# Thirty-two instead of thirty-six small unread products at the start of TensorE's program

## The chip, the core and the metric

The kernel runs on one core of a Trainium2 chip. The metric is device time in microseconds (us) for one launch, the median of several runs. A core has five engines with a queue of instructions each: TensorE (PE, matrix products; its weight loads are listed apart as PEld), VectorE (DVE), ScalarE (ACT), GpSimd (POOL) and SyncE (SP), which here only issues transfers (DMA).

## What is computed

Two stages in a row. The first is a linear attention over 4 batches, 4 heads, 1088 positions and 32 channels, with a feature map of products of two small projections:

```
phi(x) = (S1 x) outer (S2 x), flattened         # r = 8, so 64 features
kv  = sum_s phi(k)_s v_s ;  z = sum_s phi(k)_s
out = (phi(q) kv) / (phi(q) z + 1e-06)
```

The second is a gated layer with a mix over positions, on x = the attention's output with its heads joined (4 x 1088 x 128):

```
h = relu(x @ w_in)                              # 128 -> 1024
u, v = h[:512], h[512:]
v_n = (v - mean(v)) / sqrt(var(v) + 1e-06)
v_s = w_spatial @ v_n + b_spatial               # 1088 x 1088, over positions
out = (u * v_s) @ w_out                         # 512 -> 128
```

## The kernel before, in words

The 1088 positions are 9 tiles of 128 (the last half full). The large product with `w_spatial` is done for each batch and each of 4 blocks of 128 channels in three pieces of 424, 332 and 332 positions; float32 accuracy comes from splitting both factors in a high and a low part, so one product is three matrix products (lines 1123, 1125, 1132). ACT makes the high parts by a copy that rounds, DVE or POOL subtract them for the low parts. The weights `w_in`, `w_out`, `S1`, `S2` arrive as 64-bit numbers and DVE turns them into float32 with integer operations (lines 643 to 656).

The order of every engine's work is fixed before anything runs: a planner walks the operations with estimated costs, led by two written lists (ORDER, from line 69, and THEN, from line 100). In the first 50 us of its estimated time it also puts unread products (`fill`, line 605, the product at line 608) where it expects TensorE to wait. The planner sees the operation of this change as one item of a fixed cost, 1300 ns (line 603).

The start matters for this change. On DVE a tile `z9` is set to zero with two rows of ones (lines 591, 592). TensorE then runs 5 unread products 128x128 of it (N_WARM, line 596), and one operation that consists of many small ones (line 601): they write 32x32 results into a bank that is overwritten later, and take their place among four columns of the array in turn.

```
def small():                                                                        # line 598
    for i in range(N_SMALL):
        q = 32 * (i % 4)
        nc.tensor.matmul(wps[q:q + 32, :32], z9[:, q:q + 32], z9[:, :32],
                         start=True, stop=True, tile_position=(0, q))
op("PE", 1300, f4=True, fn=small, r=[z9], w=[wps], due=0)                            # line 603
```

Behind them in TensorE's queue come one fill and then the first products that matter, `project` (line 747): the keys (tiles `kt`, loaded by SP) times `sk`, the converted S1 and S2. Their results go by ACT (line 752) and DVE (line 754) into the features `kp`. Then 8 fills, the third group of keys, the first group of queries (tile `c`), one more fill, and the sums over keys (line 784). SP issues all transfers (line 580) in one queue; several wait until the tile that they overwrite has been read.

All products here are float32; the profile shows each of those products as two records of TensorE (the 5 of line 596 as 10, the 36 of line 601 as 72).

Of the kernel before, what the change touches and what calls it, by code (L numbers as in the profile page):

```python
# [36 lines left out]
EXP_LO = 2.0 ** -15  # L37
EXP_HI = 122879.9921875
N_WARM = 5
N_SMALL = 36  # L40


PS_BUFS = {"po": 3, "sp": 2, "pu": 1, "sd": 2}
# [456 lines left out]
def tile_kernel(ctx: ExitStack, tc: tile.TileContext, kT, qT, vA, sks, idn, msk, wT, w_in, w_out, bsp, out):  # L500
# [97 lines left out]
    def small():  # L598
        for i in range(N_SMALL):
            q = 32 * (i % 4)  # L600
            nc.tensor.matmul(wps[q:q + 32, :32], z9[:, q:q + 32], z9[:, :32], start=True, stop=True, tile_position=(0, q))
# [948 lines left out]
```

## Time and profile before

| | |
|---|---|
| device time, median of 3 runs | 325.61 us (324.69 to 326.08) |
| profiled execution, its time | 326.01 us |
| its span, first to last instruction | 324.2 us |
| granted TensorE clock, mean of the profile's record | 0.999 |
| busy PE / PEld / DVE / ACT / POOL | 317.2 / 301.8 / 226.2 / 164.8 / 64.5 us |

A busy share says how full an engine is over the span, not what the end hangs on; for the start of the program the order of time on each engine and the waits between them say more. A row of a timeline has a start, a duration, the engine, the line, the tile written and read, the shape and, behind x, the number of records that are merged in it. Idle time ahead of a row stands in brackets with what ended it.

### The profile page before, as it was taken

To read this page: it belongs to the slowest core of one execution; us is meant where nothing else is said; L and a number is where in the kernel's file an instruction comes from. 1 tells how busy PE (TensorE), PEld (TensorE's weight loads), DVE (VectorE), ACT (ScalarE), POOL (GpSimd) and SP (SyncE) were. 2 spreads that over 40 slices of the span, in tenths; PEclk is the share of its full clock that TensorE was granted. 3 is DMA by queue.
4 is the path that set the end of the run, shared out by engine and by line. 5 is a ranking of instruction groups with operands and counts; after the bars stand their busy time and mean duration, and the time that the engine had idled before them with its cause. 6 is when DMAs were issued, how large, how long until landed. Compare 5 with 4: busy or idle time off the path is not lost.

```text
span 324.2 us, 6830 instructions
## 1 busy us (share of the span) xinstructions
PE 317.2 (98%) x2636; PEld 301.8 (93%) x2636; DVE 226.2 (70%) x512; ACT 164.8 (51%) x391; POOL 64.5 (20%) x81
## 2 busy tenths in 40 slices
PE   8999999999999999999999999999999999999995
PEld 7887999899998999999899999999999999999995
DVE  3999995646799962889884658895325687439382
ACT  3499935525785626566544567462424455416040
POOL 1000005566201035321004702240001321103000
PEclk9999999999999999999999999999999999999999
DMA  7873229462010473011043115001000421000001
GB/s 237 289 243 129 53 58 337 142 209 73 21 52 20 129 230 126 2 40 31 14 120 121 61 51 168 0 2 42 3 0 0 128 64 42 2 1 2 0 1 69
DMA packets 21548, 26.82 MB, mean 83 GB/s; under 512 B 2828, under 2 KB 21260, under 8 KB 21516
## 3 DMA queue, kind: packets, MB, share of 16 engines
q1 hardware_dynamic: 21516, 26.39, 26.1%
q8 instruction: 20, 0.33, 0.4%
q14 instruction: 12, 0.10, 0.1%
HBM read 23.31 MB, written 3.06 MB: 81 GB/s over the span
## 4 chain that ended last, share of the span: by engine, by line
PE 77%; DVE 7%; ACT 6%; DMA 6%; issue 2%; SPq 1%; POOL 0%; POOLq 0%; DVEq 0%; ACTq 0%
PE sp L1123 15%; PE sp L1125 13%; PE sp L1132 13%; PE sd L1357 4%; DMA pl<-in_wT 4%; PE sp L1357 3%; PE sd L573 3%; PE sd L575 3%; PE sd L574 3%; PE pu L573 2%; PE po L574 2%; PE po L573 2%; PE pu L575 2%; PE pu L574 2%; PE po L575 2%; PE sp L1134 2%
## 5 line engine op out<-in xcount | busy, mean ns | idle before, releaser
L1123 PE MATMUL sp<-wTh,vh 128*128 128x332 f32 (+1 forms) x350 | 115.0, 329 | 0.0
L1125 PE MATMUL sp<-wTh,vl 128*128 128x332 f32 (+1 forms) x304 | 99.1, 326 | 0.0
L1123 PEld LDWEIGHTS sp<-wTh,vh 128*128 128x128 f32 x350 | 65.8, 188 | 2.6 <-issue 1.2
L1132 PE MATMUL sp<-wl,vh 128*128 128x332 f32 x192 | 59.9, 312 | 0.0
L1125 PEld LDWEIGHTS sp<-wTh,vl 128*128 128x128 f32 x304 | 57.1, 188 | 0.7
L1132 PE MATMUL sp<-wTl,vh 128*128 128x424 f32 x112 | 37.1, 349 | 0.0
L660 ACT CAST g<-u 128x332 fp32r<-128x332 f32 (+1 forms) x41 | 19.8, 490 | 32.5 <-DVE u L1160 22.3
L1132 PEld LDWEIGHTS sp<-wl,vh 128*128 128x128 f32 x192 | 36.0, 188 | 0.0
L583 DVE TENSOR_TENSOR g<-u,g 128x332 fp32r<-128x332 f32 (+1 forms) x41 | 23.1, 562 | 18.0 <-PE po L574 11.4
L1160 DVE TENSOR_TENSOR u<-sp,u 128x332 f32<-128x332 f32 (+1 forms) x43 | 22.4, 521 | 15.9 <-PE sp L1134 9.5
L933 DVE RECIPROCAL c<-c 128x384 f32<-128x384 f32 (+1 forms) x9 | 21.8, 2419 | 16.3 <-ACT c L931 16.3
L1115 ACT ACTIVATE u<-pu 128x332 f32<-128x332 f32 (+1 forms) x44 | 20.6, 469 | 22.2 <-PE pu L575 17.7
L1036 ACT CAST vh<-vt 128x384 fp32r<-128x384 f32 x36 | 17.3, 511 | 20.7 <-DVE vt L995 11.7
L902 POOL TENSOR_TENSOR pl<-pl,pl 128x384 f32<-128x384 f32 (+1 forms) x18 | 18.1, 1007 | 39.6 <-DMA pl<-qd 39.6
L959 DVE BATCH_NORM_STATS2 st<-vt 128x6 f32<-128x512 f32 x36 | 24.0, 684 | 2.2 <-ACT vt L957 1.9
L586 POOL TENSOR_TENSOR r<-pl,r 128x384 fp32r<-128x384 f32 (+1 forms) x18 | 17.7, 986 | 38.3 <-ACT r L660 36.1
L957 ACT ACTIVATE vt<-sd 128x512 f32<-128x512 f32 x36 | 21.4, 603 | 7.5 <-PE sd L575 6.7
L1038 DVE TENSOR_TENSOR vl<-vt,vh 128x384 fp32r<-128x384 f32 (+1 forms) x36 | 18.1, 512 | 5.3 <-ACT vh L1036 5.2
L1132 PEld LDWEIGHTS sp<-wTl,vh 128*128 128x128 f32 x112 | 21.0, 188 | 0.1
L724 POOL TENSOR_TENSOR wl<-pl,wTh 128x332 fp32r<-128x332 f32 x8 | 7.5, 953 | 49.8 <-ACT wTh L720 49.7
L573 PE MATMUL pu<-xh,wih 128*128 128x332 f32 (+1 forms) x48 | 16.5, 343 | 0.0
L995 DVE TENSOR_SCALAR vt<-vt,mv,sm 128x512 f32<-128x512 f32 x32 | 16.4, 557 | 0.0
(287 smaller groups left out, 668.1 us busy)
## 6 DMA issues: line engine op xcount, KB each, us to landing
pl<-in_wT SPq DMA_DIRECT2D x34, 166.0 KB
v<-in_vA SPq DMA_DIRECT2D x12, 198.0 KB
kt<-in_kT SPq DMA_DIRECT2D x12, 192.0 KB
pl<-qd SPq DMA_DIRECT2D x12, 192.0 KB
pl<-qd SPq DMA_DIRECT2D x24, 96.0 KB
c<-in_qT SPq DMA_DIRECT2D x9, 192.0 KB
wl<-in_wT SPq DMA_DIRECT2D x8, 212.0 KB
out<-u SPq DMA_DIRECT2D x6, 166.0 KB
```

The lines of the kernel that those rows point to most:

```text
L573: nc.tensor.matmul(o, ah, bh, start=start, stop=False)
L574: nc.tensor.matmul(o, ah, bl, start=False, stop=False)
L575: nc.tensor.matmul(o, al, bh, start=False, stop=stop)
L583: return lambda: nc.vector.tensor_tensor(out=o(), in0=a(), in1=bb(), op=ALU.subtract)
L933: op("DVE", 135 + 6.3 * n, lambda x32=x32, n=n: nc.vector.reciprocal(out=x32[:, :n], in_=x32[:, :n]), w=[x32])
L957: op("ACT", c_act(512, True), lambda pv=pv, t=t: nc.scalar.activation(vt[:, t], pv.ap, AF.Relu), r=[pv], w=[(vt, t)])
L959: op("DVE", 690, lambda stats=stats, t=t: nc.vector.bn_stats(out=stats.ap, in_=vt[:, t]), r=[(vt, t)], w=[stats])
L1123: nc.tensor.matmul(sp[:, :cw], vh[:, kt], wTh[:, kt, cs], start=(kt == begin), stop=False)
L1125: nc.tensor.matmul(sp[:, :cw], vl[:, kt], wTh[:, kt, cs], start=False, stop=False)
L1132: nc.tensor.matmul(sp[:, :cw], vh[:, kt], w_lo(kt, c), start=False, stop=False)
L1160: op("DVE", c_dve(cw), lambda: nc.vector.tensor_tensor(out=u.ap, in0=sp[:, :cw], in1=u.ap, op=ALU.mult), r=[sp], w=[u], lead=LEAD[1])
L1357: nc.tensor.matmul(x[:, :cw], p, q, start=i == 0 and n == 0, stop=end and i == 3 and n == 2)
```

## The change

One constant: the number of small products at line 601.

```
 N_WARM = 5
-N_SMALL = 36
+N_SMALL = 32
```

No other operation, tile or transfer changes, and neither does the planner's cost for the item. In TensorE's queue (names as the program gives them; the digits in them are running numbers, and shift by four because four instructions are gone) the start of the program reads so, - before and + changed:

```order
 L596 MATMUL sd_161<-u_87 128x128 x5
-L601 MATMUL sd_161<-u_87 32x32 x36
-L608 MATMUL po_222<-u_87 128x64
-L747 MATMUL sd_224<-sk,kt 64x2x32 x6
+L601 MATMUL sd_161<-u_87 32x32 x32
+L608 MATMUL po_218<-u_87 128x64
+L747 MATMUL sd_220<-sk,kt 64x2x32 x6
 L747 MATMUL sd_161<-sk,kt 64x2x32 x6
```

Only the count in the second row differs; the fill and the first key products stand where they stood, and apart from running numbers every row of all five engines is the same.

## Rows read from the trace of the kernel before

**Rows 1.** The page: busy time, share, instructions of each engine.

```profile
PE 317.2 (98%) x2636; PEld 301.8 (93%) x2636; DVE 226.2 (70%) x512; ACT 164.8 (51%) x391; POOL 64.5 (20%) x81
```

**Rows 2.** Windows, PE alone: stretch, length, busy (records), clock, DMA share, GB/s.

```profile
32.00:60.00 28.00, 28.00 (x186) 1.00 0.51 161
60.00:320.00 260.00, 258.84 (x2015) 1.00 0.19 56
```

**Rows 3.** Timeline of PE, first 13 us: start, duration, work.

```profile
1.32 2.50 PE L596 MATMUL sd<-u 128*128 128x128 f32 x10 [1.32 <-DVE u L592]
3.75 1.19 PE L601 MATMUL sd<-u 128*32 128x32 f32 x72
4.87 0.69 PE L608 MATMUL po<-u 128*128 128x64 f32 x2
5.49 1.30 PE L747 MATMUL sd<-sk,kt 128*64 128x64 f32 x24
6.73 2.00 PE L608 MATMUL po<-u 128*128 128x64 f32 x16
8.65 0.57 PE L747 MATMUL sd<-sk,kt 128*64 128x64 f32 x12
...
9.50 0.43 PE L608 MATMUL po<-u 128*128 128x64 f32 x2
9.87 1.53 PE L784 MATMUL pu<-v,kp 128*32 128x33 f32 x144
12.02 0.88 PE L833 MATMUL po<-u,kp 128*128 128x128 f32 x6 [0.62 <-DVE kp L754]
```

**Rows 4.** Chain that ended last, its start: start, length, what.

```profile
3.82 1.12 PE sd L601 x72
4.94 0.62 PE po L608 x2
5.56 1.23 PE sd L747 x24
6.80 1.93 PE po L608 x16
8.72 0.52 PE sd L747 x12
9.25 0.23 SPq L580
...
12.88 3.00 DMA wl<-in_wT
```

**Rows 5.** Timeline of DVE, the end of `sk` and the first `kp`.

```profile
4.81 0.23 DVE L656 TENSOR_TENSOR sk<-sk 128x64 f32<-128x64 f32 x1
6.72 0.95 DVE L754 TENSOR_TENSOR kp<-ka,sd 128x768 f32<-128x768 f32 x1 [1.68 <-ACT ka L752]
```

**Rows 6.** Line 747, first 10 us: its queue's waits on transfers, min/median/max ns.

```profile
L747 PEldq EVENT_SEMAPHORE  x3: 51/51/51, 4.6 to 7.9; - x3
```

**Rows 7.** Waits of the first 10 us: total, times, longest; then SP's.

```profile
ACT ka L752 <- PE sd L747: 6.0, 3, 4.2
...
DVE kp L754 <- ACT ka L752: 1.9, 2, 1.7
...
SPq L580 <- PE sd L747: 1.9, 1, 1.9
```

**Rows 8.** Groups of PE by form, windows 5.45:5.95, 6.4:6.72, 6.72:8.6: busy, mean ns.

```profile
L747 PE MATMUL sd<-sk,kt 128*64 128x64 f32 x8 | 0.7, 328 | 0.0
...
L747 PE MATMUL sd<-sk,kt 128*64 128x64 f32 x13 | 0.7, 249 | 0.0
...
L608 PE MATMUL po<-u 128*128 128x64 f32 x16 | 2.0, 278 | 0.0
L747 PE MATMUL sd<-sk,kt 128*64 128x64 f32 x4 | 0.3, 222 | 0.0
```

**Rows 9.** Windows, all engines: stretch, busy each, clock, DMA share, GB/s.

```profile
8.00:9.00 1.00, 1.00 (x18) 0.93 (x19) 0.96 (x3) 0.00 (x0) 0.00 (x0) 1.00 1.03 340
9.00:10.00 1.00, 1.00 (x37) 0.86 (x36) 0.80 (x2) 0.58 (x3) 0.00 (x0) 1.00 0.15 52
10.00:11.00 1.00, 1.00 (x124) 1.00 (x123) 1.00 (x2) 0.00 (x0) 0.00 (x0) 1.00 0.86 287
```

**Rows 10.** Waits of PE from 11 us on: total, times, longest.

```profile
PE sd L573 <- ACT vt L957: 0.5, 1, 0.5
PE po L574 <- DVE xl L583: 0.5, 1, 0.5
```

## The prediction

> **What bounds the kernel now.** I read the page's busy line first: TensorE is busy for 317.2 of 324.2 us and no other engine for more than DVE's 226.2 [rows 1]. By the windows it has no gap from 32 to 60 us, and 258.84 busy us in the 260 from 60 to 320 [rows 2]. What is saved at the start and reaches 32 us therefore reaches the end, if nothing between absorbs it: behind its wait at 12 us TensorE waits little, 0.5 us each at the two longest [rows 10].
>
> Second, TensorE's timeline at the start [rows 3]. It shows 10 records of line 596 from 1.32, the 72 records of the 36 small products from 3.75, two of a fill from 4.87, the first key products from 5.49, eight fills from 6.73, and so on without a wait until 12.02, where TensorE waits 0.62 us for DVE. Third, the chain that ended last: it runs through the small products themselves (1.12 us for 72 records), the fill, the key products and the fills, leaves TensorE at 9.25 for SP's queue, and comes to the loads of `w_spatial`, 3.00 us from 12.88 [rows 4]. So the edited item is on the path.
>
> **The change part by part.** Four products go, so 8 of 72 records. By the chain, 72 records take 1.12 us, 15.5 ns each; 8 of them are 0.124 us. The figure includes the start of the item and is, if anything, a little high.
>
> The Trainium skill, in "TensorE: Matmul & The Clock Gate" (section "Wait — 56ns, not 53.3ns?"), says that one matrix product never starts less than about 25 ns behind the one before, however small. By that page the estimate would be 8 x 25 = 0.20 us. The trace disagrees with 15.5 ns a record [rows 4], products in different columns of the array, and the measurement decides.
>
> Does the next work start earlier by that much? The fill reads only `z9` and is ready. The first key product needs `sk`, which DVE finishes at 4.81 + 0.23 = 5.04 [rows 5], and its keys: the three waits on transfers in its queue took 51 ns each, the first at 4.6, and found what they waited for [rows 6]. It started at 5.49 and would now start at 5.37, 0.33 us behind `sk`. So no stall appears in place of the removed products. A removal of up to about 0.45 us would still be covered.
>
> Who profits? ACT's first `ka` waited 4.2 us for these products, DVE's first `kp` 1.7 us for `ka`, and one transfer of SP's queue 1.9 us for the key products at 8.65 [rows 7]. All three were released by TensorE last and move with it. SP's is the one that counts: while it waits, the transfers nearly run dry, with a share of 0.15 from 9 to 10 us between 1.03 and 0.86 on either side [rows 9]. They take up again as soon as TensorE lets go, so the loads at 12.88 move too.
>
> Less than the whole 0.124 us may arrive, because of the clock. The windows print a clock of 1.00 everywhere, but the records say otherwise: the same key products have a mean of 328 ns from 5.45 to 5.95, 249 ns from 6.40 to 6.72 and 222 ns from 8.6 on [rows 8]. I read this as TensorE at 1.2 GHz at first and at 2.4 GHz from about 6.4 on, after it had been at work from 1.32 with no long hole. If the moment of the rise stays where it is, the 0.124 us won ahead of it is filled with other work at 1.2 GHz that would else have been done at 2.4 GHz, in no less than half the time. At least half of the gain stays: 0.06 us. If the rise moves along with the work, it is the whole 0.12 us. I take 0.06: nothing in the rows ties the rise to the number of products. If some load or conversion between 12 and 32 us hides the shift, the gain is 0; that is the lower end without a new loss.
>
> The sum: the profiled execution took 326.01 us, 1.8 us of it outside the span of 324.2, and stands 0.4 us above the median of 325.61. Less 0.06 it would be 325.95; on the median, 325.61 - 0.06 = 325.55 us. That is 0.02%. The runs of before differ among themselves by 1.39 us, twenty times as much, and 0.5% (1.63 us), about what a measurement of this kernel can tell from no change, lies far above any of the terms.
>
> **The rivals.** First, the clock rises later: the four products were part of the activity that brings TensorE to 2.4 GHz, and without them the rise slips. The place is the stretch from 6.4 us on, now at 222 ns a key product and 16 fill records in 1.93 us. For it: the small products are on the path only to keep TensorE at work, and they stand right ahead of the rise. Against it: nothing is left empty, since the fill and the key products simply come 0.12 us sooner, and from 5.37 until 6.4 TensorE has as much to do as before. The price: the two fill records at 4.87 took 0.62 us until the next item, those at 9.50 took 0.37, a ratio of 1.7, and twice is the most that the two levels of the clock allow. The 16 records of 1.93 us would take 1.3 to 1.9 us longer, and they delay the key products at 8.65, on which SP's transfers wait. If the clock stayed low until the wait at 12.02, everything from 6.4 to 11.4, 5.0 us, would take up to as much again; some of it would hide in the 0.62 us wait, and DVE's conversions would cover a part. So a slip costs 1.3 to 4 us; I take 2.0, which gives 327.6 us, slower by 0.6%. It decides when the slip is over about 3.3 us, as one us at the lower level loses about half a us of work, and 1.63 are needed.
>
> The Trainium skill speaks to this in the same page's section "What's actually happening": the hardware watches activity over time and does not count instructions, and the same kernel rises at different points from run to run. By that the count of small products would not matter here. The rows show one execution and one rise, so they neither confirm nor refute it.
>
> Second, the clock rises earlier: key products and fills stream 64 columns where the small ones stream 32, and they come sooner. Were the clock full from 5.37 instead of 6.4, a us of work at the lower level would shrink by up to half, 0.5 us on top of 0.12: 325.0 us, which is 0.2% and still within the bound. Nothing in the rows speaks for it but the order of the records.
>
> Third, the shift is absorbed. DVE is the engine that TensorE waits for at 12.02, and between 12 and 32 us ACT, DVE and the loads take turns. If DVE's own work set the time there and not what TensorE and SP hand it, 325.6 us would stay. Against it is the dry stretch of the transfers from 9 to 10 us [rows 9].
>
> **How the numbers follow.** I give the forecast (a gain of 0.06 to 0.12 us that arrives) 0.66, absorbed 0.18, the earlier rise 0.08, the later rise 0.08. The first three lie within 0.5%. The spread of the runs of before can carry a median beyond the bound without any cause, for 0.03 to 0.04 on either side: I put 0.04 to faster; slower is that 0.03 and 0.05 of the later rise (the rest are slips under 3.3 us), 0.08 together, and 0.88 is left for same. The likeliest case has 325.55 us. Its own range is that of the runs of before, 324.7 to 326.1; widened by the earlier rise below and short slips above it is 324.6 to 326.5.
>
> **What would show it.** In the changed kernel's timeline, 64 records of line 601 should last 1.00 us in the chain, the fill start near 4.75, the first key product near 5.37 with no idle time ahead of it, `kp` on DVE near 6.60, the key products of 8.65 between 8.53 and 8.60, and the SP transfer behind them as much earlier. From 32 us on every row should stand earlier by 0.06 to 0.12 us. The means of line 747 should fall from about 328 to 222 ns near 6.4 us, as before. The forecast is wrong if those means stay high past 7 us, if 16 fill records take over 2.5 us, or if the key products wait for `sk`.

## The result, and the profile after

The changed kernel takes 327.0 us (median of 22 runs, 325.18 to 330.01) against 325.3 us (22 runs, 324.19 to 328.75). The ratio of the mean times is 1.0069, with a 95% interval of 1.0042 to 1.0096 (the medians alone give 1.0052); the ratios below are of this kind. It is slower, and 327.0 lies above the range of 324.6 to 326.5. The runs are also spread wider: 9 of the 22 lie above 327.5 us, and 1 of 22 did before. The other 13 have a median of 326.4 us, 1.1 us above the kernel before.

The profiled execution took 327.09 us with a span of 325.3 (before: 326.01 and 324.2). Its start on TensorE, start and duration first as in [rows 3]:

```profile
3.75 1.08 PE L601 MATMUL sd<-u 128*32 128x32 f32 x64
4.76 0.69 PE L608 MATMUL po<-u 128*128 128x64 f32 x2
5.38 1.55 PE L747 MATMUL sd<-sk,kt 128*64 128x64 f32 x24
6.87 2.19 PE L608 MATMUL po<-u 128*128 128x64 f32 x16
8.98 0.57 PE L747 MATMUL sd<-sk,kt 128*64 128x64 f32 x12
```

The first key product stands at 5.38, 0.11 us earlier, as worked out. By 8.98 the start is 0.33 us later than before: the 24 records of line 747 and the fills took longer, since the clock rose later in this execution, among the fills (the 16 fill records need 2.11 us to the next item, against 1.92 in [rows 3]). That is not what costs 1.1 us of span. A constant lag of 0.33 us stays until 62 us, where the wait of 0.5 us for `xl` [rows 10] does not occur, and TensorE is then 0.35 us ahead of the kernel before. The loss comes at one place. First before, then after, TensorE near the third burst of line 784 (the sums over keys of the third batch):

```profile
115.31 0.31 PE L575 MATMUL pu<-xh,wil 128*128 128x332 f32 x1
115.55 1.67 PE L784 MATMUL sd<-v,kp 128*32 128x33 f32 x144
117.15 0.42 PE L573 MATMUL pu<-xh,wih 128*128 128x332 f32 x1
```

```profile
114.96 0.31 PE L575 MATMUL pu<-xh,wil 128*128 128x332 f32 x1
115.20 1.47 PE L784 MATMUL sd<-v,kp 128*32 128x33 f32 x125
117.91 0.38 PE L784 MATMUL sd<-v,kp 128*32 128x33 f32 x19 [1.24 <-issue]
118.22 0.42 PE L573 MATMUL pu<-xh,wih 128*128 128x332 f32 x1
```

Ahead of the burst the changed kernel leads by 0.35 us (114.96 for 115.31), behind it the kernel lags by 1.07 (118.22 for 117.15), and at the last products by 1.09 (321.05 for 319.96). In the middle of one operation TensorE stands still for 1.24 us with no semaphore to wait for: the trace says "issue". The waits of TensorE from 30 us on (total, times, longest) are these in the changed kernel:

```profile
PE sd L784 <- issue: 1.2, 1, 1.2
PE sp L1123 <- issue: 0.7, 1, 0.7
PE po L574 <- DVE g L583: 0.2, 1, 0.2
```

What does TensorE lack? The transfers have a queue of their own for instructions, q8, of which section 3 of the page lists 20 loads with 0.33 MB. By windows, the kernel before has one of them from 112 to 114.9 us, ahead of the burst, and none from 114.9 to 117.7, while the burst runs; the changed kernel has none from 112 to 115 and one from 115 to 117, when the burst is under way (queue, loads, MB, share of the 16 engines; before, then after):

```profile
q8 instruction: 1, 0.02, 2.2%
```

```profile
q8 instruction: 1, 0.02, 4.0%
```

So the reading at this point was: the program's instructions come in blocks, and taking away 16 instructions in front (four products of two records each, a record with its weight load; 6830 to 6814 recorded instructions on all engines) moved the edge of a block against the work. A burst of 72 small products (144 records) consumes its instructions in 1.6 us, and a block asked for as late as its start arrives too late.

The packets of q8 in the traces bear this out more closely than the windows. In the changed kernel the load runs from 115.36 to 116.64, and TensorE goes on at 117.91, 1.27 us behind its end. In the six traces of this case with a hole in this burst, and the three with a hole between 11.8 and 18.9 us (below), TensorE goes on 1.27 to 1.55 us behind the end of a load on q8, whether the hole is 1.24 or 4.46 us long. In the six traces without a hole in this burst the load had ended 2.1 to 3.6 us before TensorE came to the same place in its stream (before the change: 113.89, and 116.61). What starts a load is not shown: in three traces of the changed kernel this one starts behind TensorE's weight load 1134, 1176 and 1237.

### The profile page after: what moved, and what is told of

It is laid out like the page before. It is cut to its first block, busy times and chain, and to the rows that moved or that the text cites. A ratio compares the mean times of both kernels' runs of the same rounds, so it can differ in the third digit from the quotient of the medians.

```text
span 325.3 us, 6814 instructions
## 1 busy us (share of the span) xinstructions
PE 317.2 (98%) x2628; PEld 302.1 (93%) x2628; DVE 225.6 (69%) x512; ACT 164.9 (51%) x391; POOL 63.7 (20%) x81
## 4 chain that ended last, share of the span: by engine, by line
PE 92%; DVE 2%; issue 1%; SPq 1%; ACT 1%; DMA 1%; DVEq 0%
PE sp L1123 18%; PE sp L1125 15%; PE sp L1132 15%; PE sd L1357 4%; PE sd L573 3%; PE sp L1357 3%; PE sd L574 3%; PE sd L575 3%; PE pu L573 3%; PE po L573 2%; PE pu L574 2%; PE pu L575 2%; PE sp L1134 2%; PE po L575 2%; PE po L574 2%; PE sd L747 2%
## 5 line engine op out<-in xcount | busy, mean ns | idle before, releaser
L1123 PE MATMUL sp<-wTh,vh 128*128 128x332 f32 (+1 forms) x350 | 114.9, 329 | 0.7 <-issue 0.7
L583 DVE TENSOR_TENSOR g<-u,g 128x332 fp32r<-128x332 f32 (+1 forms) x41 | 22.2, 541 | 18.0 <-PE po L574 13.4
L1160 DVE TENSOR_TENSOR u<-sp,u 128x332 f32<-128x332 f32 (+1 forms) x43 | 22.4, 521 | 15.5 <-PE sp L1134 8.7
```

Of the source, the lines that this page charges most:

```text
L583: return lambda: nc.vector.tensor_tensor(out=o(), in0=a(), in1=bb(), op=ALU.subtract)
L1123: nc.tensor.matmul(sp[:, :cw], vh[:, kt], wTh[:, kt, cs], start=(kt == begin), stop=False)
L1160: op("DVE", c_dve(cw), lambda: nc.vector.tensor_tensor(out=u.ap, in0=sp[:, :cw], in1=u.ap, op=ALU.mult), r=[sp], w=[u], lead=LEAD[1])
```

## The experiments

The theories: L, instructions arrive late in the burst; A, the clock rises late or falls, which is the first rival of the prediction; B, the time shift itself brings a wait. Each group of kernels below had runs of the kernel before on the same chip.

**Four kernels to separate clock, time and place.** The changed kernel again:

> The changed kernel once more, for more traces. Theory A (the clock's rise): most executions lie within 1 us of the kernel before and some 3 to 4 us above it, so a median 0.3 to 1% above; in the trace the program's first 13 us are later by as much as the key and fill records take at the low clock, and from 32 us on all rows stand later by a constant. Theory B (a wait that the shift by 0.1 us causes later): the start is 0.1 us earlier in every trace and the time is lost at one wait between 12 and 60 us, of the same size in every execution, about 1 to 2 us.

Median 327.84 us, ratio 1.007 (1.0039 to 1.0102); 7 of 12 above 327.5 us. The profiled execution, at 330.07, has both losses. Its TensorE:

```profile
6.87 3.68 PE L608 MATMUL po<-u 128*128 128x64 f32 x16
10.47 0.91 PE L747 MATMUL sd<-sk,kt 128*64 128x64 f32 x12
```

```profile
PE sd L784 <- issue: 2.1, 1, 2.1
PE sp L1123 <- issue: 0.6, 1, 0.6
```

16 fill records in 3.68 us in place of 2.00 [rows 3], and the second keys at 10.47 for 8.65: the clock stayed at its lower level into the burst that starts at 12.57 (the trace's first record of the clock, at 1.00, stands at 14.16). It is the first rival, seen in an execution: by 26 us it is 2.3 us behind the first trace of the changed kernel and 2.6 us behind the kernel before. The hole in the burst adds 2.1 us. So A and L both occur, and B's constant wait of one size does not: 1.24 us here, 2.1 there.

The fills at 128 columns, with 32 small products:

```
-        nc.tensor.matmul(homes[tag, slot][:, :64], z9.ap, z9[:, :64], start=True, stop=True)
+        nc.tensor.matmul(homes[tag, slot][:, :128], z9.ap, z9[:, :128], start=True, stop=True)
```

> The changed kernel (32 small products) with the unread fills at 128 columns in place of 64. At the low clock 128-column records start 213 ns apart, and a fill record is expected to take as long as before, since its weights are loaded for as long. Theory A: TensorE is busier in the same time, the clock rises early in all executions, no time above 327 us, median 325.0 to 325.4. Theory B: order and times of the start are those of the changed kernel, so 327 us as there.

327.0 us, ratio 1.0052 (1.0028 to 1.0075), lowest 326.45. The clock did not rise earlier in its trace (first record at 7.52 us, for 7.28 in the changed kernel), so the fills did not do what they were widened for. Still, only 3 of 12 lie above 327.5, the bulk does not come down to 325.3, and the trace has the hole of the burst (1.4 us by its waits): the loss is there without a late rise, and A alone is not its cause.

The same line with `:16`, and 36 small products:

> The kernel before (36 small products) with the fills at 16 columns in place of 64: as long by their weight loads, but less work in them. Theory A: the rise comes late in more executions, as in the changed kernel or worse: median 326.5 to 329 us. Theory B: nothing changes, 325.3 us, since no item moves by more than 0.05 us.

326.02 us, ratio 1.0019 (0.9993 to 1.0045), no difference shown. The trace has no hole in the burst, but a fall of the clock (stretch, length, busy and records, clock, DMA, GB/s):

```profile
6.60:9.90 3.30, 3.30 (x58) 1.00 0.83 267
10.00:13.30 3.30, 3.26 (x150) 0.50 0.91 296
13.40:16.00 2.60, 2.60 (x31) 1.00 0.93 310
```

Theory A had 326.5 to 329 here and missed: a fall to 1.2 GHz from 10 to 13.3 us happened and cost little. The wait for DVE at 12 us took up a part (line 833 starts at 12.00, for 12.02 before); by 24 us the execution is 0.6 us behind the kernel before (line 573 at 24.70, for 24.11), and at the burst it is 0.14 us ahead (115.41, for 115.55).

24 small products (`N_SMALL = 24`):

> 24 small products in place of 32: eight more gone. Theory A: the share of executions that rise late grows, median 327 to 329.5 us. Theory B: the start moves another 0.11 us, and a wait that takes the place grows by the same 0.1 us at most: 327.1 us; if the loss was a coincidence of two transfers, it may be gone, 325.3 us.

327.76 us, ratio 1.0057 (1.0025 to 1.0089); 6 of 12 above 327.5. The hole stands in the burst (1.6 us), and the profiled execution has a late rise as well, with 3.68 us for the 16 fill records. Counted in the traces, the hole lies behind TensorE's 1237th weight load in the changed kernel, with the wide fills and in this one, although other work stands there in this one: its burst breaks behind record 141 and not 125. A number that stays while the work moves through it is what L says.

**The four products put back at another place.** Behind the first sums over keys TensorE waits 0.62 us for DVE [rows 3]. There N_PAD unread products are put:

```
-N_SMALL = 36
+N_SMALL = 32
+N_PAD = 4
...
+            for i in range(N_PAD if not b and g == 2 else 0):
+                q = 32 * (i % 4)
+                nc.tensor.matmul(kv[q:q + 32, 256:288], z9[:, q:q + 32], z9[:, :32],
+                                 start=True, stop=True, tile_position=(0, q))
```

> 32 small products in front, and the four that were taken away are put back behind the first sums over keys (line 784), where TensorE waits for DVE anyway: from there on every instruction has the number in TensorE's stream that it had before. Theory L (instructions arrive late): the hole of 1.2 to 2.1 us in the second batch's... third burst of line 784 near 117 us, seen in all kernels with fewer instructions in front, is gone, and so is the 0.7 us one near 173; executions in which the clock rises in time take 324.3 to 326.4 us as before. Theory A (clock) on top: a third of the executions still lies at 327 to 329 us, since the front is that of the changed kernel; median about 325.7. A rival, that the shift in time by 0.1 to 0.3 us causes the hole: it stays, since the start is as in the changed kernel, median 327.

325.31 us, ratio 0.9976 (0.9956 to 0.9996), all 12 runs between 324.15 and 325.99. The burst is whole:

```profile
114.04 1.72 PE L785 MATMUL sd<-v,kp 128*32 128x33 f32 x144
115.69 0.42 PE L574 MATMUL pu<-xh,wih 128*128 128x332 f32 x1
```

The hole and the loss are gone with the same front as in the changed kernel, so the front's time (B) and its products (A) do not make them by themselves. The third of late executions that A promised did not come either. Of the wait near 173 us, which was to go too, the 0.4 us are left that the kernel before has.

With many more instructions in the same place:

> 36 small products in front as before, and 34 more in the same place behind line 784, about 0.64 us of work in a wait of 0.62 us: 136 instructions more ahead of everything that follows. Theory L: hole near 117 us absent, and the one of 0.4 us near 171 that the kernel before has goes too, since the loads of instructions are asked for at other places; nothing above the kernel before in clock. 324.9 us median, few executions above 327. Rival (time): the same as before or up to 0.1 us later, 325.4 us.

> 36 in front and 24 behind line 784, 96 instructions more. Theory L: the place where TensorE runs out moves, and falls into the burst of line 784 near 69 us (a hole of 0.5 to 1.3 us there), none near 117 and none or a small one near 171: 325.5 to 326.3 us. Rival (time): as the kernel with 34, to 0.1 us.

> 32 in front and 38 behind line 784: from there on the stream of the kernel with 36 and 34. Both theories of holes give the same from 12 us on; what is left is the front. Theory A: some third of the executions 2 to 4 us above the kernel with 36 and 34, the others 0 to 0.1 us below it. If the clock had no part: no execution above 327 us and 0.1 us below it.

These three missed by far: 333.73 us (ratio 1.0231, 1.0192 to 1.0271), 333.14 (1.0186, 1.0138 to 1.0235, without its longest run, 336.26) and 334.49 (1.025, 1.0199 to 1.0302), with 6 runs each. The products do not fit in a wait of 0.62 us; they prolong the first burst, and TensorE runs out of instructions in the middle of them or, with 24, six records behind them. TensorE in the kernel with 36 and 34, and then its windows:

```profile
11.16 0.65 PE L791 MATMUL pu<-u 128*32 128x32 f32 x54
16.27 0.43 PE L791 MATMUL pu<-u 128*32 128x32 f32 x13 [4.46 <-issue]
16.63 1.54 PE L837 MATMUL po<-u,kp 128*128 128x128 f32 x6
```

```profile
5.00:11.60 6.60, 6.10 (x266) 1.00 0.98 335
11.70:16.20 4.50, 0.10 (x13) 0.86 1.00 346
16.30:25.20 8.90, 8.90 (x68) 0.50 0.49 148
25.30:30.00 4.70, 4.70 (x35) 1.00 0.01 2
```

The hole is longer here, 4.46 us (2.88 with 24 and 2.97 with 38 products), while the transfer engines are full (share 1.00) with the loads of `w_spatial`; that this is the reason was not tried. In the hole the clock falls to 0.50, and it stays there until 25.2. That the hole near 171 us would be gone held for all three; the one foretold near 69 us in the kernel with 24 came as 0.2 us near 81. The kernels with 34 and 38 say nothing on the front, as they hardly differ from each other in what costs most.

The holes now known lie behind weight loads 349 (with 34 and 38; 348 with 24), 856 (with 24), 1237, and 1745 (near 171 us, present before the change too). The distances are 507, 381 and 508, so 4, 3 and 4 times 127 to within one, and 127 weight loads with their 127 records of products are 254 instructions. The Trainium skill, in "Runtime: NRT & Kernel Launch" (section "Instruction fetch mechanics"), says that instructions are refilled in blocks of 256, the next one while the current one runs. The distances agree, with a few waits that take up instructions too. The page also says that the cost of crossing a block is mostly hidden; the holes of 1.2 to 4.5 us are not hidden, and the measurement decides.

**Again, side by side.** The changed kernel, the same with 4 behind the first burst, and two that go on in the same manner:

> The changed kernel beside e10, in turn with it on one chip. Theory L (instructions arrive late near 117 us): executions without a late rise at 326.2 to 327, one hole of 1.2 us or more there in the trace. Theory A (late rise in some executions): about a third at 328 to 330.

> 32 in front, 4 behind line 784, again. Theory L: no hole near 117 us, executions with an early rise at 324.2 to 326. Theory A, if the front alone decides on the rise: as many late ones as in e9, now at 327 to 329, and the none of 12 that e5 had was chance. If the number of instructions decides on the rise too: none again.

> 28 in front and 8 behind line 784: from there on every instruction has the number it had before. Theory L: no hole near 117 us; the start is 0.21 us earlier than before the change where the clock has risen before it matters, so 325.1 us or 0.1 to 0.2 below the kernel before. Theory A: some 30 to 50% at 327 to 329, median then 325.5 to 327.

> 24 in front and 12 behind line 784. Theory L: no hole near 117 us (the kernel with 24 alone had 1.6 us there); 0.3 us earlier at the start, 325.0 us without late rises. Theory A: late ones as in the kernel with 24 alone, five to seven of twelve, at 327 to 328.5 us. Together they say that the difference between 24 alone and this kernel is the hole, and what is left against the kernel before is the clock.

The changed kernel: 328.74 us, ratio 1.0079 (1.0042 to 1.0115), 8 of 12 above 327.5. With 4 behind: 325.4, 0.9985 (0.9962 to 1.0008), none above 325.98. With 28 and 8: 325.27, 0.9991 (0.9959 to 1.0023); with 24 and 12: 325.47, 1.0015 (0.998 to 1.005); 3 of 12 above 327.5 in either. None of the last three has a wait for instructions near 117 us, though 24 alone had. The trace of the changed kernel shows where its runs near 329 come from, TensorE in time and then in windows:

```profile
114.23 1.46 PE L784 MATMUL sd<-v,kp 128*32 128x33 f32 x125
117.75 0.54 PE L784 MATMUL sd<-v,kp 128*32 128x33 f32 x19 [2.05 <-issue]
118.22 0.65 PE L573 MATMUL pu<-xh,wih 128*128 128x332 f32 x1
```

```profile
112.00:115.50 3.50, 3.50 (x138) 1.00 0.88 258
115.50:117.70 2.20, 0.19 (x24) 1.00 0.80 234
117.75:121.10 3.35, 3.35 (x28) 0.50 0.43 116
121.20:124.00 2.80, 2.80 (x19) 1.00 0.42 122
```

A hole of 2.05 us, and behind it the clock at 0.50: a product of line 573 takes 0.65 us for 0.42, and the nine products from it on take 3.03 us, for 1.69 in the kernel before. The clock of A takes part, but behind L's hole, in a stretch where TensorE has nothing to spare. It does not follow each time: in the execution of 330.07 us the hole was 2.06 us long and the clock stayed at 1.00 behind it.

The mean clock over an execution, which is listed for each run of the changed kernels, tells the two kinds of long executions apart. It is 0.994 in this one and in the one of 329.24 us below, whose traces show a fall behind the hole; it is 1.0 in those of 330.07 us and, with 24 in front, 329.09 us, whose traces show a late rise, as nothing is recorded of the clock ahead of its first rise. By this sign the 24 of 46 runs of the changed kernel above 327.5 us are 10 with a fall (0.994 or 0.995) and 14 without (0.998 and more), for which a late rise is the likely reason. Of the kernel before, none of the 104 runs with a listed clock has a mean under 0.998, and 7 of all 126 runs lie above 327.5 us.

**Ahead of the burst or anywhere?** In all of these the total number of products changed with the number ahead of the burst. The last kernel has 32 in front and four unread products behind the third burst:

```
+            for i in range(4 if b == 2 and g == 2 else 0):
+                q = 32 * (i % 4)
+                nc.tensor.matmul(kv[q:q + 32, 256:288], f[:, 0, q:q + 32], f[:, 0, :32],
+                                 start=True, stop=True, tile_position=(0, q))
```

> 32 in front, and the four products are put back behind the third burst of line 784 (at about 117 us) and not ahead of it. The program has as many products as before, but up to that burst every instruction of TensorE has the number that it has in the changed kernel. Theory L (what counts is the number of instructions ahead of the burst): the hole of 1.2 to 2.3 us inside the burst stays, median 326.5 to 328.5 us, some executions at 328 to 330. Rival (four products more, wherever they stand, or the total, cure it): no hole there, 325.4 us as with the four products behind the first burst.

326.55 us, ratio 1.0029 (1.0001 to 1.0058), 4 of 12 above 327.5. The hole is there, behind weight load 1237 again, and in the profiled execution (329.24 us) longer than in any other of these bursts:

```profile
114.78 1.47 PE L784 MATMUL sd<-v,kp 128*32 128x33 f32 x125
119.13 0.49 PE L784 MATMUL sd<-v,kp 128*32 128x33 f32 x18 [2.89 <-issue]
```

It breaks the burst behind record 125, as in the changed kernel. So the number of instructions ahead of the burst decides on the hole, and the total does not. Three of the 12 runs lie at 324.64 to 324.86 us, below all 46 of the changed kernel; whether they had the hole no trace shows.

## Why the prediction was wrong, step by step

- **The duration of the removed products** (0.124 us): 0.11 measured, right, and the 15.5 ns a record were a little high, as said. The next work did not wait: the key products began at 5.38 (foretold 5.37), and `kp` on DVE at 6.61 (6.60):

```profile
6.61 0.95 DVE L754 TENSOR_TENSOR kp<-ka,sd 128x768 f32<-128x768 f32 x1 [1.51 <-ACT ka L752]
```

  The room of 0.45 us holds only at the lower clock: in the trace with 28 in front the clock had risen by 4.7 us (two fill records in 0.43 us), and the key products waited 0.40 us for `sk`.

- **At least half of the gain stays, with the rise where it is**: not in this execution. The moment of the rise differs between executions of one kernel: in the trace before it fell among the key products [rows 8], and in the three of the changed kernel among the fills, behind 12 us, and ahead of the key products (first record of the clock at 6.37 us before, and at 7.28, 14.16 and 5.08). One trace was taken for the rule. The 16 fill records are the row to read it by: 1.92 us before, 2.11 and 3.6 in two executions of the changed kernel.
- **"What is saved at the start and reaches 32 us therefore reaches the end, if nothing between absorbs it"**: this is the step that failed. The sum held only the waits that the kernel before has. That every later instruction changes its number in TensorE's stream, by 16, was not in the sum; it is an effect of the edit that stands in no row of the order. It cost 1.24 to 2.06 us in the three traces of the changed kernel, as TensorE ran out of instructions in the middle of a burst. Alone it would have stayed within about 0.3%: the 13 of 22 runs below 327.5 us have a median of 326.4 us, for 325.3 before. What the median has above that comes with the 9 others, 3 with a fall of the clock and 6 without, which are likely to have risen late. The kernel before showed the price in a row that [rows 10] leave out:

```profile
PE po L574 <- issue: 0.4, 1, 0.4
```

  It stands near 171 us and is of the same kind: a load on q8 ends at 170.35, and TensorE goes on at 171.72. The instruction queue was in section 3 of the page.
- **The first rival** (a later rise, 327.6 us, 8 in 100) came out near the time, but that is in part luck: its late rise is one part of the loss, and the hole, which it does not have, is the other. A late rise adds 2.3 us to the execution of 330.07 us, and by the mean clock it is the likely reason in 14 of 46 runs of the changed kernel. But with the same front and the four products put back, 24 of 24 runs stay under 326 us, so the number of products in front does not decide on it alone.
- **The third rival** (absorbed): not shown. In the profiled execution 0.7 us are won back at 62 us, as DVE's `xl` comes in time there; but that wait is missing in the trace with 36 in front and narrow fills too, so it differs between executions and is not to be put down to the change.
- **Same within 0.5%, at 88 in 100**: the spread of before was read as noise of the clock, and no case was kept for an effect far from the edited place.

What stays open: how often the clock rises late with each front, and why. Runs above 327.5 us were 7 of 126 with 36 small products, 24 of 46 with 32 (14 of them without a fall), 0 of 24 with 32 and 4 behind, 3 of 12 each with 28 and 8 and with 24 and 12. These numbers give no order of the fronts, and why the four products behind the first burst take the late executions away as well is not known. It is open too what starts a block's load and why it takes as long as it does; that the transfer engines were at a share of 1.00 in the longest hole was seen, but not tried by itself.

The version to keep is 32 in front and 4 behind the first burst: 0.9976 (0.9956 to 0.9996) and 0.9985 (0.9962 to 1.0008) of the kernel before, so at most 0.4% faster, and perhaps not at all.

## What to carry to other kernels

An edit that only takes instructions out moved, in this kernel, all that follow against the blocks in which the engine's instructions are loaded. Where a program has bursts of very short instructions, look in the trace for waits on "issue" there, before and after, and if one appears, put as many cheap instructions back in a wait ahead of the burst, and no more than fit there: 24 to 38 products in a wait of 0.62 us cost some 8 us here. Judge a change of this size by many runs and more than one trace.

## What the runs showed of the hardware that was not expected

- TensorE can run dry of instructions for 1.2 to 2.9 us inside a burst of 144 records that needs 1.6 us, and for 2.9 to 4.5 us near the start, where other transfers fill the engines. The distances between the places are multiples of 127 weight loads, to within one, and TensorE goes on 1.27 to 1.55 us behind the end of a load of instructions on q8.
- Such a hole can be followed by a clock of 0.50 (2.05 us idle, then 0.50 from 117.75 to 121.10), which adds 1.3 us over the next nine products; behind a hole of 2.06 us in another execution the clock stayed at 1.00.
- The windows print a clock of 1.00 for the start of the program, where the records' durations (328 ns, later 222, for one kind of product [rows 8]) show the lower level.
